# Dividing layer one's first and fifth mixing product into seven, with the shared sums made earlier

## The chip, the cores and the metric

The kernel runs on one core of a Trainium2 chip. The metric is the device time of one execution in microseconds (us); of several runs the median is given. TensorE (PE in the profile) multiplies matrices, VectorE (DVE) and ScalarE (ACT) work elementwise, GpSimd (POOL) does elementwise work and issues some DMAs, and SyncE (SP) issues the other DMAs in one queue.

## The reference

Two layers with the same weights, over a sequence of 2048 tokens with 512 features, all in fp32. Each layer is a linear attention block A and a gated mixer B, both behind a layer norm and with a residual.

```
def A(x):                      # 32 heads of 16
    q, k, v = split(x @ wqkv)
    pq, pk = phi(q), phi(k)    # phi(t) = (t + 1 if t > 0 else exp(t)) + 1e-6
    kv, z = pk^T v, sum_s pk
    return concat_heads((pq @ kv) / (pq @ z + 1e-6)) @ wo

def B(x):                      # 1792 features, halves of 896
    z = gelu(x @ w_in)
    z1, z2 = z[:, :896], layernorm(z[:, 896:])
    g = w_sp @ z2 + b_sp       # w_sp: 2048 x 2048, mixes the tokens
    return (z1 * g) @ w_out

for layer in (1, 2):
    x = x + A(layernorm(x))
    x = x + B(layernorm(x))
```

The term that this study is about is `w_sp @ z2`, called the mixing here.

## The kernel before

Every fp32 operand of a large matmul is split into a high part (ScalarE copies it as fp32r) and a low part (VectorE subtracts); a product is three matmuls, high by high, high by low and low by high (`mm3`, lines 121 to 125, and `acc` in the mixing, lines 1049 to 1053). The order in which each engine gets its instructions is the order of the program, written out by hand. Buffers come from four pools with first-in-first-out lists (class `Slots`): 22 pages of 128 x 512, 6 `quads` of 128 x 2048, 4 `bigs` of 128 x 3584 and 8 banks of PSUM. In the profile these are pg, qd, bg and bank; z tiles hold the normalised z2, 128 tokens each.

A layer has four stages.

- First half (class `P1`), 16 token tiles: layer norm statistics (`stats`: VectorE, then three small operations on GpSimd, lines 190 to 193), normalising on ScalarE (line 199), a store and load through DRAM that, with a blockwise transpose on VectorE (line 251), turns the tile (class `Turn`), and its split (`T_high`, `T_low`). Then the projections K and Q, phi (lines 323 to 327), and the product of x with phi(k) (`Gmm`); step s does K of tile s-1, Q of s-1 and `Gmm` of s-2, 36 matmuls. Before the first tile TensorE is given filler matmuls (`idle` in `start`, line 415).
- `transition`, and the token steps (class `P2`, 18 steps): attention's output (`c`), the next layer norm, the turned x and its split (`d_high`, `d_low`), z2 (`e`, with the Gelu in `e2`, line 667) and z1 (`f`), which is stored to DRAM.
- The mixing (class `P4`): w_sp is a 2 x 2 block matrix, and seven block products (Winograd's form) make up the result. They are called P1 to P7 here and run in the order P2, P1, P6, P7, P4, P5, P3. A product has 8 steps of 24 matmuls (P2, P1, P4, P5) or of 18. Per step `sp` splits the fetched block of w_sp (`wsp`, high on ScalarE in line 885, low on VectorE in line 886) and the z operand (`zsp`), two steps ahead; `fetch` loads four steps ahead. `evac` takes a product's banks out into the big tiles on VectorE. `gate` (line 1089, GpSimd) multiplies a finished unit of g with z1, loaded by `ask`; `tick` issues one gate a step in undivided products.
- The output product with w_out (`o`), to whose steps the next layer's start is joined. P3's steps also load and split w_out (`wpiece`).

`DIVIDED` names the products that are themselves taken as seven products of quarter blocks: 14 steps of 12 matmuls (`mm_div`, `evac_div`), whose z operands are summed and split on VectorE and ScalarE (`zsum`, `zpart`) four steps ahead. Before, this is layer two's P2 and P4.

Sums of blocks of w_sp are needed by both layers (class `Sums`). `tick` makes two of them on GpSimd (`add`, line 805) from loaded blocks and stores them (line 800); the blocks are loaded one call ahead by `fetch`, and if none is loaded `tick` loads them at once. There are 32 such calls, 14 in layer one's token steps and the rest in its mixing. Before, the divided products' sums (`halve`, line 783) are all made in layer one's mixing: 16 copies from DRAM to DRAM on SP, then 16 accumulating DMAs issued by GpSimd (line 795), each behind the newest weight split (`behind` adds such a wait, `self.mark` is that ScalarE instruction).

## Time and profile before

| | |
|---|---|
| time, median of 3 runs | 1388.18 us (1385.9 to 1389.07) |
| the profiled execution | 1386.75 us, span 1384.9 us |
| TensorE busy | 1376.4 us, 6182 matmuls |
| VectorE, ScalarE, GpSimd busy | 893.1, 587.6, 396.7 us |
| DMA | 248.76 MB, mean 180 GB/s |
| layer one's mixing | 351.4 to 624.8 us |
| layer two's mixing | 1041.1 to 1304.6 us |

The profile is one execution. A line of a group gives the source line, the engine and the operation, the tiles written and read, the shape and the count; then busy time, the mean of one in ns, and the idle time just before them with what ended it. A line of the order of time gives the start and the length in us, and in brackets the idle time before the instruction and what released it. A row of stretches gives for each engine the busy time and in brackets the number of instructions.

### The profile page before, as it was taken

Reading aid. Unit: us, or ns where it says so; the run is one execution under the profiler, and the core shown is the slowest. Engines: PE = TensorE matmul, PEld = TensorE weight load, DVE = VectorE, ACT = ScalarE, POOL = GpSimd, SP = SyncE. Lnnn points to the kernel's source line nnn. Section 1 sums busy time; section 2 is a strip of 40 time slices with the busy share of each in tenths; the row PEclk is TensorE's granted clock in tenths of the full one; section 3 lists DMA queues with packets and bytes.
Section 4 is the critical chain, followed back from the end, with each engine's and each line's share of the span. In section 5 each row is a group of like instructions: output and inputs, shape, how many; then the busy total and the mean of one; then the engine's idle time right before and its main releaser. Section 6 shows DMA issues by size and latency. Waiting matters only on the chain.

```text
span 1384.9 us, 17460 instructions
## 1 busy us (share of the span) xinstructions
PE 1376.4 (99%) x6182; PEld 1149.0 (83%) x6182; DVE 893.1 (64%) x1331; ACT 587.6 (42%) x893; POOL 396.7 (29%) x506
## 2 busy tenths in 40 slices
PE   9999999999999999999999999999999999999998
PEld 7888888888888888878888888888888888878887
DVE  6665877752578665674566658775438667886632
ACT  6664534434323333341256646443346333633410
POOL 3333455543466201342012334432100020021300
PEclk9999999999999999999999999999999999999999
DMA  5632267775999877893735322555346445454432
GB/s 159 202 115 62 92 213 258 250 240 193 329 309 317 302 248 190 228 266 114 228 112 185 115 61 95 175 179 168 114 148 202 137 167 155 147 186 149 161 123 91
DMA packets 148344, 248.76 MB, mean 180 GB/s; under 512 B 12448, under 2 KB 51104, under 8 KB 148000
## 3 DMA queue, kind: packets, MB, share of 16 engines
q1 hardware_dynamic: 145952, 239.26, 52.2%
q0 software_dynamic: 2304, 8.39, 3.4%
q8 instruction: 48, 0.79, 0.2%
q14 instruction: 40, 0.33, 0.1%
HBM read 179.70 MB, written 84.67 MB: 191 GB/s over the span
## 4 chain that ended last, share of the span: by engine, by line
PE 91%; DVE 4%; DMA 2%; ACT 2%; issue 1%; POOL 1%; SPq 0%; ACTq 0%; DVEq 0%; POOLq 0%
PE bank L125 18%; PE bank L124 18%; PE bank L123 18%; PE bank L1052 11%; PE bank L1053 11%; PE bank L1051 11%; DMA pg<-in_wout_dram 1%; DVE qd L886 1%; PE bank L515 1%; PE bank L526 0%; ACT qd L885 0%; DVE st L186 0%; PE bank L211 0%; DMA pg<-in_wqkv_dram 0%; DVE pg L112 0%
## 5 line engine op out<-in xcount | busy, mean ns | idle before, releaser
L1052 PE MATMUL bank<-qd,pg 128*128 128x512 f32 x784 | 305.5, 390 | 1.5 <-DVE qd L886 1.5
L1053 PE MATMUL bank<-qd,pg 128*128 128x512 f32 x784 | 305.3, 389 | 0.0
L1051 PE MATMUL bank<-qd,pg 128*128 128x512 f32 x784 | 305.1, 389 | 0.0
L886 DVE TENSOR_TENSOR qd<-qd,qd 128x1024 fp32r<-128x1024 f32 x124 | 166.7, 1345 | 135.3 <-ACT qd L885 135.0
L885 ACT ACTIVATE qd<-qd 128x1024 fp32r<-128x1024 f32 x124 | 131.3, 1059 | 184.4 <-PE bank L1053 158.9
L1052 PEld LDWEIGHTS bank<-qd,pg 128*128 128x128 f32 x784 | 147.1, 188 | 33.9 <-DVE qd L886 3.5
L1053 PEld LDWEIGHTS bank<-qd,pg 128*128 128x128 f32 x784 | 147.2, 188 | 31.1 <-DVE pg L925 0.7
L1051 PEld LDWEIGHTS bank<-qd,pg 128*128 128x128 f32 x784 | 147.1, 188 | 31.0 <-ACT pg L923 0.4
L1089 POOL TENSOR_TENSOR bg<-bg,pg 128x512 f32<-128x512 f32 x56 | 83.8, 1512 | 279.6 <-DVE bg L1099 121.0
L125 PE MATMUL bank<-qd,pg 128*128 128x512 f32 x384 | 149.8, 390 | 0.1
L190 POOL TENSOR_SCALAR rs<-mv 128x1 f32<-128x1 f32 x96 | 27.3, 284 | 343.5 <-DVE mv L188 342.8
L199 ACT ACTIVATE pg<-pg,nb,rs 128x512 f32<-128x512 f32 x63 | 51.2, 812 | 172.1 <-POOL nb L193 172.0
L123 PE MATMUL bank<-qd,pg 128*128 128x512 f32 x288 | 112.4, 390 | 0.1
L124 PE MATMUL bank<-qd,pg 128*128 128x512 f32 x288 | 112.2, 390 | 0.0
L805 POOL TENSOR_TENSOR pg<-pg,pg 128x512 f32<-128x512 f32 x64 | 93.8, 1466 | 55.0 <-DMA pg<-in_wsp_dram 46.0
L123 PE MATMUL bank<-bg,qd 128*128 128x448 f32 x256 | 94.2, 368 | 0.4 <-ACT qd L109 0.4
L125 PE MATMUL bank<-bg,qd 128*128 128x448 f32 x256 | 93.6, 365 | 0.1
L124 PE MATMUL bank<-bg,qd 128*128 128x448 f32 x256 | 93.6, 366 | 0.0
L125 PE MATMUL bank<-qd,bg 128*128 128x512 f32 x224 | 87.5, 391 | 0.0
L124 PE MATMUL bank<-qd,bg 128*128 128x512 f32 x224 | 87.4, 390 | 0.0
L123 PE MATMUL bank<-qd,bg 128*128 128x512 f32 x224 | 87.2, 389 | 0.0
L123 PE MATMUL bank<-wo,qd 128*128 128x512 f32 x224 | 87.1, 389 | 0.0
(137 smaller groups left out, 2557.9 us busy)
## 6 DMA issues: line engine op xcount, KB each, us to landing
qd<-s SPq DMA_DIRECT2D x64, 512.0 KB, 3.8
qd<-in_wsp_dram SPq DMA_DIRECT2D x44, 512.0 KB, 4.2
pg<-in_wsp_dram SPq DMA_DIRECT2D x64, 256.0 KB, 4.8
s<-pg SPq DMA_DIRECT2D x64, 256.0 KB, 4.5
pg<-x SPq DMA_DIRECT2D x64, 256.0 KB, 2.9
z<-pg SPq DMA_DIRECT2D x56, 256.0 KB, 2.8
pg<-z SPq DMA_DIRECT2D x56, 256.0 KB, 4.3
x<-pg SPq DMA_DIRECT2D x48, 256.0 KB, 2.6
```

Of the source, the lines that this page charges most:

```text
L123: nc.tensor.matmul(out, ah, bh, start=start, stop=False)
L124: nc.tensor.matmul(out, ah, bl, start=False, stop=False)
L125: nc.tensor.matmul(out, al, bh, start=False, stop=stop)
L190: nc.gpsimd.tensor_scalar(rs, mv[:, 1:2], LN_EPS, None, op0=OP.add)
L199: nc.scalar.activation(y, x, AF.Identity, bias=nb, scale=rs)
L805: nc.gpsimd.tensor_tensor(t, a, b, op=OP.add)
L885: self.mark = nc.scalar.activation(w[:, 0], r, AF.Copy)
L886: nc.vector.tensor_sub(w[:, 1], r, w[:, 0].bitcast(F32))
L1051: m(out, h[:, o], w[:, 0, j, :], start=start, stop=False, skip_group_check=True)
L1052: m(out, h[:, o], w[:, 1, j, :], start=False, stop=False, skip_group_check=True)
L1053: m(out, l[:, o], w[:, 0, j, :], start=False, stop=stop, skip_group_check=True)
L1089: nc.gpsimd.tensor_tensor(u, u, z1, op=OP.mult)
```

## The change

- Layer one's P2 and P4 are divided too.
- The shared sums start in layer one's first half: eight calls of `tick` in its steps 2 to 9, with two big tiles cut into sheets as their buffers (class `Sheets`), 14 in the token steps as before, none in P2, ten in P1 and P6.
- The divided products' sums are made earlier: the copies for P2 in steps 14 to 17 of the first half, its accumulations in token steps 4 to 11 (behind that step's Gelu), the copies for P4 in token steps 9 to 16, its accumulations in P6 and the start of P7.
- A gate waits for the newest weight split.
- `evac` takes the two delta banks of P1 and P5 out after the others; in layer one P1's banks are taken out ahead of the next split.
- At the end of P7 the weight split of one more step is issued ahead of `evac`. Counters (`made`, `zmade`) keep a split from being made twice.
- `Turn.pre` issues the VectorE transpose of the next tile at the end of a step of the first half.
- The last four filler matmuls are half as wide.

```diff
@@ -50,7 +50,25 @@
             self.free_list.append(n)
 
 
-DIVIDED = ((), ("P2", "P4"))
+DIVIDED = (("P2", "P4"), ("P2", "P4"))
+
+
+class Sheets:
+
+
+    def __init__(self, slots, n):
+        self.slots = slots
+        self.tiles = [slots.get([P, NF, 512]) for _ in range(n)]
+        self.free_list = deque(t[:, f, :] for t in self.tiles for f in range(NF))
+
+    def get(self, shape):
+        return self.free_list.popleft()
+
+    def put(self, *sheets):
+        self.free_list.extend(sheets)
+
+    def close(self):
+        self.slots.put(*self.tiles)
 
 
 @with_exitstack
@@ -217,7 +235,7 @@
 
         def __init__(self, name, by_pe, always=False, inbank=False):
             self.name, self.by_pe, self.always, self.inbank = name, by_pe, always, inbank
-            self.held, self.d, self.raw = {}, {}, {}
+            self.held, self.d, self.raw, self.made = {}, {}, {}, {}
 
         def turned(self, i):
 
@@ -245,12 +263,19 @@
                 if self.always:
                     pages.put(s)
                 return b, banks
+            self.pre(i)
+            return self.made.pop(i)
+
+        def pre(self, i):
+
+            if i in self.made or i not in self.raw:
+                return
             r = self.raw.pop(i)
             home = banks if self.inbank else pages
             y = home.get([P, 4, P])
             nc.vector.transpose(y.rearrange("p c (t m) -> p m c t", m=4), r.rearrange("p (m c j) -> p m c j", m=4, c=4))
             pages.put(r)
-            return y, home
+            self.made[i] = y, home
 
 
     class P1:
@@ -410,9 +435,9 @@
             nc.vector.tensor_copy(m, f)
             b = banks.get(PAGE)
 
-            def idle(n):
+            def idle(n, w=512):
                 for _ in range(n):
-                    nc.tensor.matmul(b, ones, m, start=True, stop=True)
+                    nc.tensor.matmul(b[:, 0:w], ones, m[:, 0:w], start=True, stop=True)
 
             idle(10)
             self.ln_a(0)
@@ -420,7 +445,7 @@
             self.ln_b(0)
             self.wk.piece()
             self.T_high(0)
-            idle(4)
+            idle(4, 256)
             banks.put(b)
             pages.put(m, f)
             self.T_low(0)
@@ -467,10 +492,24 @@
                     self.Gmm(s - 2)
                 if s == NT + 1:
                     self.late_phi()
+                if self.L == 0:
+                    if s == 2:
+                        sums.slots = Sheets(bigs, 2)
+                    if 2 <= s < 10:
+                        sums.tick(s < 9)
+                    if s == 10:
+                        sums.store()
+                        sums.slots.close()
+                        sums.slots = pages
+                    if 14 <= s < 18:
+                        sums.halve(2 * s - 28, None)
+                        sums.halve(2 * s - 27, None)
                 if s == 6:
                     self.wv, self.wo = (quads.get([P, 4, 512]) for _ in range(2))
                     nc.sync.dma_start(self.wv, wqkv[:, 1024:1536].rearrange("(c p) f -> p c f", p=P))
                     nc.sync.dma_start(self.wo, wo_d.rearrange("(c p) f -> p c f", p=P))
+                if s in range(3,NT-1):
+                    self.turn.pre(s + 1)
                 if s > 3 and side:
                     side.popleft().piece()
                 if s > 2 and side:
@@ -664,7 +703,7 @@
         def e2(self, i):
             z = ztag(i, [P, FH], f"z{self.L}")
             for j, b in enumerate(self.eb):
-                nc.scalar.activation(z[:, j * HF:(j + 1) * HF], b, AF.Gelu_apprx_tanh)
+                self.mark = nc.scalar.activation(z[:, j * HF:(j + 1) * HF], b, AF.Gelu_apprx_tanh)
                 banks.put(b)
 
         def e3(self, i):
@@ -747,8 +786,13 @@
                 self.fnext = []
                 w1.piece(True)
                 w1.fetch()
-                if self.L == 0 and s > 4:
-                    sums.tick()
+                if self.L == 0:
+                    if s > 4:
+                        sums.tick(s < NT + 2)
+                    if 4 <= s < 12:
+                        sums.halve(12 + s, self.mark)
+                    if 9 <= s < 17:
+                        sums.halve(s - 1, None)
                 if s >= NT + 1:
                     self.p4.fetch(s - NT - 1)
             self.e4(NT - 1)
@@ -847,6 +891,7 @@
                 else:
                     self.steps += [(p, k) for k in range(HT)]
             self.tmp, self.bank = {}, {}
+            self.made = 0
             self.beta = self.delta = None
             self.wout = {}
             self.asked, self.gq = deque(self.gates()), deque()
@@ -873,9 +918,11 @@
             self.raw[g] = t
 
         def sp(self, g):
-            self.wsp(g)
-            if g < len(self.steps) and self.steps[g][0] not in self.div:
-                self.zsp(g)
+            while self.made < min(g + 1, len(self.steps)):
+                self.wsp(self.made)
+                if self.steps[self.made][0] not in self.div:
+                    self.zsp(self.made)
+                self.made += 1
 
         def wsp(self, g):
             if g >= len(self.steps):
@@ -1086,20 +1133,13 @@
         def gate(self, n, f):
             z1 = self.z1.pop((n, f))
             u = self.unit(n, f)
-            nc.gpsimd.tensor_tensor(u, u, z1, op=OP.mult)
+            behind(nc.gpsimd.tensor_tensor(u, u, z1, op=OP.mult), self.mark)
             pages.put(z1)
 
         def evac(self, p):
 
             V, bs = nc.vector, self.bs
             gates = []
-            if p in ("P1", "P5"):
-                for j in range(2):
-                    n = 2 + j if p == "P1" else j
-                    V.tensor_add(self.unit(n, 3), self.unit(n, 3) if self.joins(p) else bs[n],
-                                 self.delta[j])
-                    gates.append((n, 3))
-                banks.put(*self.delta)
             for j in range(2):
                 a, b = 2 + j, j
                 for f in range(3):
@@ -1126,6 +1166,13 @@
                         gates.append((a, 4 + f))
                     if p in ("P2", "P4", "P3") or (p == "P7" and "P4" in self.div):
                         banks.put(q)
+            if p in ("P1", "P5"):
+                for j in range(2):
+                    n = 2 + j if p == "P1" else j
+                    V.tensor_add(self.unit(n, 3), self.unit(n, 3) if self.joins(p) else bs[n],
+                                 self.delta[j])
+                    gates.append((n, 3))
+                banks.put(*self.delta)
             self.gq.extend(gates)
 
         def wpiece(self, f):
@@ -1163,27 +1210,25 @@
             if i % 4 == 3:
                 bigs.put(self.gb[i // 4])
 
+        def zahead(self, g):
+
+            while self.zmade <= g:
+                self.zsum(self.zmade + 1)
+                self.zpart(self.zmade)
+                self.zmade += 1
+
         def run(self, nxt):
             p2 = self.p2
             self.fetch(2)
             self.sp(0)
             if self.div:
                 self.loadb()
-            ahead = deque()
+            self.zmade = 0
             if self.div:
-                self.zpart(0)
-                self.zpart(1)
-                ahead.extend([2, 3, 4, 5, 6, 7][:4 - 2])
-                self.zsum(2)
+                self.zahead(1)
             while p2.f():
-                if ahead:
-                    g = ahead.popleft()
-                    self.zsum(g + 1)
-                    self.zpart(g)
-            while ahead:
-                g = ahead.popleft()
-                self.zsum(g + 1)
-                self.zpart(g)
+                self.zahead(min(self.zmade, 3))
+            self.zahead(3)
             p2.win1.free()
             self.sp(1)
             self.fetch(3)
@@ -1192,20 +1237,25 @@
             for g in range(n):
                 p, k = self.steps[g]
                 self.fetch(g + 4)
-                evac_first = p == "P6" and k == HT - 1
+                evac_first = (p == "P6" or p == "P1" and nxt is not None) and k == HT - 1
                 div_first = p in self.div and k == 13 and p == "P4"
                 if not evac_first and not div_first:
                     self.sp(g + 2)
-                    self.zsum(g + 4 + 1)
-                    self.zpart(g + 4)
+                    self.zahead(g + 4 if p in ("P2", "P1") else g + 4)
                 self.mm(g)
                 if evac_first:
+                    if p == "P1":
+                        self.ask(3)
                     self.evac(p)
                     self.sp(g + 2)
-                if g < 19:
+                if p != "P2" or not self.div:
                     self.sums.tick()
-                if nxt is not None:
-                    self.sums.halve(g - 19, self.mark)
+                elif nxt is not None and k == 1:
+                    self.sums.store()
+                elif nxt is not None and k == 13:
+                    self.sums.fetch()
+                if nxt is not None and g >= 24:
+                    self.sums.halve(g, self.mark)
                 if g == 3 and not self.div:
                     self.loadb()
                 if p in self.div:
@@ -1227,6 +1277,8 @@
                         self.loadx(1)
                     if k == 7:
                         self.zsplit(0)
+                if p == "P7" and k == HT - 1 and self.div:
+                    self.sp(g + 3)
                 if k == HT - 1 and not evac_first:
                     self.evac(p)
             pages.put(*self.bs)
```

## The prediction

> **What bounds the kernel now.** I read the page first (busy shares, the chain that ended last, the costly groups), then busy time by stretches of the span, then the waits and the order of time around each stall. The page:
>
> ```profile
> span 1384.9 us, 17460 instructions
> PE 1376.4 (99%) x6182; PEld 1149.0 (83%) x6182; DVE 893.1 (64%) x1331; ACT 587.6 (42%) x893; POOL 396.7 (29%) x506
> PE 91%; DVE 4%; DMA 2%; ACT 2%; issue 1%; POOL 1%; SPq 0%; ACTq 0%; DVEq 0%; POOLq 0%
> L1052 PE MATMUL bank<-qd,pg 128*128 128x512 f32 x784 | 305.5, 390 | 1.5 <-DVE qd L886 1.5
> L805 POOL TENSOR_TENSOR pg<-pg,pg 128x512 f32<-128x512 f32 x64 | 93.8, 1466 | 55.0 <-DMA pg<-in_wsp_dram 46.0
> ```
>
> TensorE is busy for 99% of the span and makes 91% of the chain. The L1052 row is one of the mixing's three matmul lines (L1051 to L1053); it waited 1.5 us in all over both layers. L805 are the shared sums' adds on GpSimd, 1.47 us each, which waited 46 us for their blocks. So a matmul taken away is worth its pace, unless something else becomes late.
>
> The two layers run the same mixing, but layer two takes P2 and P4 (the first and fifth block product, in the order P2, P1, P6, P7, P4, P5, P3) as seven half-size products already. The trace of before therefore shows the changed stage once. First the matmuls of line L1051 in the mixing of layer one and of layer two, then all engines in single products. The columns after the stretch are its length, the busy time of each engine with its instruction count, TensorE's granted clock, the DMA share and GB/s.
>
> ```profile
> 351.40:624.80 273.40, 155.61 (x400) 74.92 (x400) 1.00 0.86 271
> 1041.10:1304.60 263.50, 149.52 (x384) 71.91 (x384) 1.00 0.51 167
> ```
> ```profile
> 351.40:395.10 43.70, 43.70 (x195) 36.18 (x194) 28.98 (x29) 14.75 (x19) 21.43 (x14) 1.00 0.96 333
> 395.10:438.70 43.60, 43.60 (x194) 36.12 (x193) 32.53 (x32) 12.47 (x16) 24.63 (x16) 1.00 0.93 310
> 1041.10:1079.30 38.20, 38.20 (x169) 31.33 (x169) 34.58 (x53) 24.06 (x34) 0.00 (x0) 1.00 0.67 209
> 1079.30:1122.90 43.60, 43.60 (x194) 36.12 (x193) 25.67 (x39) 12.46 (x16) 1.67 (x2) 1.00 0.39 131
> 1122.90:1155.70 32.80, 32.80 (x147) 27.15 (x146) 20.96 (x27) 11.51 (x15) 8.80 (x7) 1.00 0.51 176
> 1188.40:1228.40 40.00, 39.25 (x171) 31.30 (x169) 37.34 (x56) 24.93 (x37) 4.83 (x3) 1.00 0.54 171
> ```
>
> The first two of the second block are P2 and P1 of layer one, the other four P2, P1, P6 and P4 of layer two. Undivided P2 takes 43.7 us, divided 38.2; divided P4 40.0, because it has stalls. The reader should see what the division costs beside TensorE: VectorE works 34.6 of 38.2 us and 37.3 of 40.0, against 29.0 of 43.7 undivided. That is narrow, and it holds only while GpSimd does next to nothing (0.0 and 4.8 us there, 21 to 25 us in layer one's first two products).
>
> **The matmuls removed.** An undivided P2 or P4 has 8 steps of 24 matmuls, 192; divided it has 14 steps of 12, 168. Two products save 48, as the rows say: 400 less 384 is 16 on each of three lines. The pace is 43.7 us / 192 = 0.2276 us in the undivided product and 38.2 / 168 = 0.2274 in the divided one. 48 x 0.2274 = **-10.9 us**, all on the path.
>
> **Stalls that the change may take away.** The first blocks are TensorE's own order of time at late matmuls, then ScalarE's, GpSimd's and VectorE's beside them.
>
> ```profile
> 615.31 0.39 PE L1051 MATMUL bank<-qd,pg 128*128 128x512 f32 x1
> 616.49 0.50 PE L1052 MATMUL bank<-qd,pg 128*128 128x512 f32 x1 [0.79 <-DVE qd L886]
> ```
> ```profile
> 1194.56 0.50 PE L1052 MATMUL bank<-qd,pg 128*128 128x512 f32 x1 [0.45 <-DVE qd L886]
> ...
> 1219.64 0.50 PE L1052 MATMUL bank<-qd,pg 128*128 128x512 f32 x1 [0.30 <-DVE qd L886]
> ```
> ```profile
> 1188.68 3.62 ACT L1117 ACTIVATE bg<-bg 128x512 f32<-128x512 f32 x6 [2.64 <-DVE bg L1115]
> ```
> ```profile
> 1213.70 3.53 POOL L1089 TENSOR_TENSOR bg<-bg,pg 128x512 f32<-128x512 f32 x2 [70.24 <-DVE bg L1017]
> ```
> ```profile
> 1210.46 1.22 DVE L886 TENSOR_TENSOR qd<-qd,qd 128x1024 fp32r<-128x1024 f32 x1
> ...
> 1214.14 1.95 DVE L886 TENSOR_TENSOR qd<-qd,qd 128x1024 fp32r<-128x1024 f32 x1
> ```
>
> In layer two's P4 the stall at 1194 follows six ScalarE copies (L1117, the end of P7) that stand ahead of the next weight split; the change puts that split ahead of them. The one at 1219 follows two gates (L1089) that GpSimd began inside P4: beside them the split's low half took 1.95 us and not 1.22. The change makes a gate wait for the ScalarE half of the newest split, which holds it back until P5. Both stalls have an answer, so of the 40.0 - 38.2 = 1.8 us that P4 loses I take 1.5 back (bounds 0 and 1.8): **-1.5 us**. Queued behind a gate that waits are only GpSimd's later gates, and on SP the load into the page that it frees. The late matmul at 615, in layer one's P3, is (616.49 - 615.31) - 0.23 = 0.95 us late; it came while accumulating DMAs and P3's loads of w_out shared the DMA engines. The accumulating DMAs move ahead to P6 and P7, but P3's gates now wait for splits; I take 0.8 back (bounds +1 and -0.95): **-0.8 us**.
>
> **The sums' cold starts.** A tick that finds no loaded blocks holds GpSimd until they land. Before, this happens once, in the token steps; the rows are GpSimd, ScalarE and TensorE there.
>
> ```profile
> 191.61 2.66 POOL L805 TENSOR_TENSOR pg<-pg,pg 128x512 f32<-128x512 f32 x2 [3.07 <-DMA pg<-in_wsp_dram]
> ```
> ```profile
> 195.64 0.82 ACT L199 ACTIVATE pg<-pg,nb,rs 128x512 f32<-128x512 f32 x1 [8.07 <-POOL nb L193]
> ```
> ```profile
> 196.28 0.39 PE L125 MATMUL bank<-qd,pg 128*128 128x512 f32 x1
> 197.03 0.47 PE L123 MATMUL bank<-bg,qd 128*128 128x448 f32 x1 [0.36 <-ACT qd L109]
> ```
> ```profile
> L795 POOL DMA_DIRECT2D hP<-in_wsp_dram x8 | 6.8, 853 | 84.9 <-ACT qd L885 84.9
> ```
>
> GpSimd waits 3.07 us for the blocks, the layer norm's statistics stand behind the adds, ScalarE's normalising behind them, and a matmul is 0.52 us late. The change keeps this cold tick and puts an accumulating DMA behind its adds (0.85 us of GpSimd, L795) ahead of the same statistics. Its wait for the step's Gelu costs nothing: on GpSimd it stands behind the statistics of that Gelu's output. **+0.8 us** (bounds 0 and 3; the upper end if the blocks land later beside the accumulation).
>
> The second cold tick is new, in layer one's first half at its second step.
>
> ```profile
> 29.04 0.22 POOL L190 TENSOR_SCALAR rs<-mv 128x1 f32<-128x1 f32 x1 [2.12 <-DVE mv L188]
> ```
> ```profile
> 25.69 0.38 SPq L235 DMA_DIRECT2D xt<-pg  x1
> ```
> ```profile
> pg<-in_wsp_dram SPq DMA_DIRECT2D x64, 256.0 KB, 4.8
> ```
> ```profile
> 35.37 0.69 DVE L112 TENSOR_TENSOR pg<-bank,pg 128x512 fp32r<-128x512 f32 x1
> ```
> ```profile
> 40.14 0.39 PE L123 MATMUL bank<-qd,pg 128*128 128x512 f32 x1
> ```
>
> The loads go out behind the store at 25.69, the third about 27; landing takes 4.8 us, so both adds (2.66) are done near 34.4, and the statistics that ran at 29.04 start 5.4 us late. From them a serial chain (normalise, phi, turn, split) ends in the L112 of 35.37, done at 36.06, which the matmul at 40.14 needs: 4.1 us of slack. 5.4 - 4.1 = 1.3; I take **+1.0 us** (bounds 0 and 3). The later ticks load one step ahead (36 matmuls, 8.2 us, against 4.8) and are hidden. A tick's store waits on SP for the adds; behind it stand the next x load and turned load, needed a step later.
>
> **The traffic that moves.**
>
> ```profile
> 18.20:82.00 63.80, 63.80 (x284) 52.79 (x283) 43.44 (x74) 44.33 (x75) 19.35 (x32) 1.00 0.52 163
> 115.00:148.00 33.00, 33.00 (x160) 26.58 (x159) 19.83 (x39) 15.50 (x28) 8.89 (x8) 1.00 0.13 43
> 194.00:352.00 158.00, 157.57 (x723) 135.28 (x722) 93.00 (x141) 64.19 (x104) 77.59 (x111) 1.00 0.72 237
> ```
> ```profile
> q0 software_dynamic: 2304, 8.39, 3.4%
> ```
>
> Eight ticks with 8.4 MB of loads and stores go to the stretch from 18 to 82 us. At 333 GB/s for a share of 0.96 they are 24 us of DMA, 3 a tick and 0.38 of the stretch: 0.52 becomes 0.90. Eight copies of 0.5 MB go to the end of the first half (share 0.13), eight to the token steps, with eight accumulations (3.4% of 1384.9 us / 16 = 2.9 us each; a token step's 60 matmuls are some 13): 0.72 becomes about 0.94, more for three steps where both fall. No matmul waited at 0.96 in layer one's P2, so I cost this at nothing. If the cover is gone, the token steps' turned loads come late. VectorE has room for the adds: 43.4 of 63.8 us, plus 16 times the 0.73 us by which a busy GpSimd lengthened a split, is 55.
>
> The Trainium skill, "SBUF — State Buffer", section "Who interferes with whom", says that a VectorE instruction with two SBUF inputs and a GpSimd one that reads SBUF exclude each other for the whole instruction. The rows agree that they hurt each other, by 0.73 us and not by the whole of a gate. Its outcome is a rival below.
>
> In layer one's mixing the accumulations for P4 fall in P6 and early P7, ten ticks in P1 and P6, and P1's results are now taken out, by eight VectorE operations, ahead of the next split. For all that together: **+0.8 us** (bounds 0 and 4). The turn issued at the end of the step before, the two delta banks taken out last in P1 and P5, and the counters for splits and parts change an order only where today no matmul waits, and the next step's 18 to 36 matmuls cover them: 0.
>
> **The warm-up.**
>
> ```profile
> 7.22 1.16 PE L415 MATMUL bank<-pg,ones 128*128 128x512 f32 x4
> 8.53 0.51 PE L123 MATMUL bank<-qd,pg 128*128 128x512 f32 x1
> ```
>
> Four half-width filler matmuls save some 0.45 us, but the first real matmul already starts after their end, waiting for its split: 0 (bounds -0.4 and +0.5).
>
> **Sum:** -10.9 - 1.5 - 0.8 + 0.8 + 1.0 + 0.8 = -10.6 us. The profiled execution took 1386.75 us (span 1384.9 and 1.85 around it), so 1376.15; the median of the runs, 1388.18, lies 1.43 above it: **1377.6 us**.
>
> **Rivals.**
> *P6 becomes bound by DMA* (15%). Layer two's P6 has a share of 0.51, 16.7 us of 32.8. Six accumulations add 17.6 and two ticks about 6: 40 us, 7.5 too many. Fetched blocks have two steps (36 matmuls, 8.2 us) less some 4.8 of landing, 3.4 us, so 4.1 us would be lost: 1381.7. For it: the sum of shares. Against: P1 of layer one ran at 0.93 without a wait, and the accumulations may be what waits.
> *Slower: the ticks starve the layer norm in the first half* (9%). If the adds' blocks land later than 8.2 + 4.1 = 12.3 us, every tick delays the statistics, and GpSimd, ScalarE and TensorE in turn. Slower than before by 0.2% needs 13.4 us of new loss, 1.7 us in each of eight steps, a landing of 14.0. At three times today's 4.8 (14.4) it would be 2.1 x 8 = 17 us: 1394. For it: a share near 0.90 on average, with 2 MB of weights in the middle. Against: the 64 loads of the 4.8 us ran in stretches with shares of 0.72 to 0.96.
> *VectorE is shut out for the whole of each add* (6%), the rule named above. 16 adds in P1 of layer one at 1.47 us are 23.5 us on top of layer two's P1, 25.7 of 43.6, 5.6 over; in the first half 43.4 + 23.5 is 3.1 over 63.8; 8.7 lost: 1386.3, no change. Against: layer one's P1 today, VectorE 32.5 and GpSimd 24.6 of 43.6, with no wait.
> That the matmuls are not saved is excluded by the count.
>
> **How the numbers follow.** The forecast's case has 70%. About 0.2%, 2.8 us, is what a measurement of this kernel tells from no change. The forecast and the first rival are faster (0.85), the third the same (0.06), the second slower (0.09). Low end: all stalls gone, nothing new, -10.9 - 1.8 - 0.95 - 0.4 = -14.1, 1374.1, less 1.6 for the runs' spread. High end: the first rival, 1381.7, with the two cold ticks some 1.2 us dearer each, 1384.
>
> **What would show it.** Right: 384 matmuls on each mixing line in layer one and a mixing of 262 to 264 us there; layer two's P4 near 38.2; waits of 0.5 to 2 us near 40 and 197. Wrong: TensorE waiting in every step from 24 to 82 us, in P6, or VectorE over 38 us in layer one's divided products.

## The result and the profile after

The changed kernel takes 1402.32 us in the median of four runs (1400.12 to 1403.28), the kernel before 1387.10 in four. The ratio is 1.0106, with a 95% interval from 1.0088 to 1.0125: 15 us slower, where 10.6 us faster was forecast. The profiled execution took 1400.12 us.

The page of the changed kernel: its span, the busy shares, TensorE's granted clock in 40 slices, and the chain that ended last, by engine and by line.

```profile
span 1398.3 us, 17506 instructions
PE 1373.8 (98%) x6134; PEld 1142.9 (82%) x6134; DVE 937.7 (67%) x1411; ACT 611.4 (44%) x939; POOL 420.1 (30%) x506
PEclk9999999899999999999999999999999999999999
PE 82%; DMA 7%; DVE 5%; ACT 2%; POOL 1%; issue 1%; SPq 1%; DVEq 0%; ACTq 0%; POOLq 0%
PE bank L141 15%; PE bank L143 15%; PE bank L142 15%; PE bank L1099 12%; PE bank L1098 12%; PE bank L1100 12%; DMA yt<-pg 2%; DMA s<-pg 2%; DMA pg<-xt 1%; DVE st L204 1%; DMA qd<-s 1%; DVE pg L130 1%; ACT pg L217 1%; PE bank L554 1%; DMA z<-pg 0%
```

The 48 matmuls are gone (6134, before 6182), TensorE is busy 2.6 us less, and yet the span is 13.4 us longer. DMA had 2% of the chain and has 7%, and the chain names the transfers: the store of the turned tile in the token steps (yt), the store of a finished sum (s). One slice of the clock row, the eighth (245 to 280 us), is not a 9.

The stretches tell where. First the kernel before, then the changed one, each with the first half and transition, layer one's token steps, layer one's mixing and layer two's mixing. The columns are the length, busy time and count of PE, PEld, DVE, ACT and POOL, the granted clock, the DMA share and GB/s.

```profile
2.30:159.10 156.80, 156.53 (x704) 127.98 (x705) 104.89 (x184) 94.69 (x160) 50.63 (x77) 1.00 0.41 128
159.10:351.50 192.40, 191.97 (x892) 165.68 (x891) 120.90 (x189) 79.49 (x129) 95.45 (x137) 1.00 0.69 224
351.50:624.80 273.30, 272.51 (x1202) 225.09 (x1201) 190.02 (x218) 94.82 (x123) 101.19 (x73) 1.00 0.86 271
1041.20:1304.60 263.40, 262.65 (x1154) 215.72 (x1153) 198.34 (x288) 117.67 (x164) 33.76 (x24) 1.00 0.51 167
```
```profile
2.30:160.90 158.60, 156.35 (x705) 127.12 (x705) 106.90 (x184) 95.05 (x161) 75.27 (x93) 1.00 0.64 206
160.90:375.10 214.20, 199.95 (x890) 169.54 (x889) 117.69 (x199) 80.71 (x134) 97.30 (x142) 0.96 0.80 242
375.10:640.50 265.40, 263.42 (x1154) 215.65 (x1154) 224.36 (x287) 116.97 (x164) 81.75 (x52) 1.00 0.70 223
1056.80:1318.20 261.40, 261.40 (x1153) 216.21 (x1152) 209.04 (x288) 117.91 (x164) 49.07 (x24) 1.00 0.51 168
```

Layer one's mixing is 7.9 us shorter and layer two's 2.0, the first half is 1.8 longer, and the token steps are **21.8 us longer**; the remaining stretches are unchanged. In the token steps TensorE stands still for 14.3 us (before 0.4), and nearly the same number of matmuls takes 8.0 us longer. Only there is the granted clock below 1.00.

The largest group of TensorE's waits in the whole span (total, times, longest), and the order of time around the longest: TensorE, then VectorE, ScalarE, and the issues of SP and GpSimd. The last fence is the same store and load in the kernel before.

```profile
PE bank L141 <- ACT qd L127: 13.9, 5, 6.7
```
```profile
238.25 0.40 PE L143 MATMUL bank<-qd,pg 128*128 128x512 f32 x1
245.40 0.74 PE L141 MATMUL bank<-bg,qd 128*128 128x448 f32 x1 [6.74 <-ACT qd L127]
...
233.25 1.10 DVE L276 STREAM_TRANSPOSE pg<-pg 128x512 f32<-128x512 f32 x1 [3.15 <-DMA yt<-pg]
243.60 1.08 DVE L276 STREAM_TRANSPOSE pg<-pg 128x512 f32<-128x512 f32 x1 [5.49 <-DMA s<-pg]
...
244.71 0.63 ACT L127 ACTIVATE qd<-pg 128x512 fp32r<-128x512 f32 x1 [4.65 <-DVE pg L276]
...
226.73 0.37 SPq L253 DMA_DIRECT2D yt<-pg  x1
233.22 0.32 SPq L118 DMA_DIRECT2D pg<-yt  x1
...
234.01 0.93 POOL L839 DMA_DIRECT2D hP<-hP  x1
```
```profile
220.21 0.37 SPq L235 DMA_DIRECT2D yt<-pg  x1
222.69 0.32 SPq L100 DMA_DIRECT2D pg<-yt  x1
```

All of the 13.9 us end with the split of the turned tile (L127), the operand of z2's matmuls (L141). Read the longest wait backwards: the split waits for the transpose at 243.60, the transpose for a DMA, and before that the load could not go out until the store had landed, 6.5 us after it was issued; before it was 2.5. The transpose at 243.60 is put down to the store of a sum (s): the load it reads had landed at 236.0, 2.8 us after its issue, but the page it writes to came free only when that store was done, 8 to 9 us after its issue at 234.6, beside the accumulating DMA (hP<-hP) issued at 234.01. The transpose at 233.25 turns another tile (attention's) and is put down to yt's store in the same way.

The second longest wait (3.29 us, at 277.75) ends with a sum's store too. In the other three (1.23 us at 199.62, 0.81 at 227.28, 1.85 at 305.19) the split stands on ScalarE right behind a normalising that waited for GpSimd's statistics, in the last two of them because VectorE was late behind such pages. The lines give what VectorE's transposes waited for (total, times, longest), first in the kernel before (180 to 300 us), then in the changed one (190 to 320 us).

```profile
DVE pg L251 <- DMA yt<-pg: 0.7, 2, 0.5
```
```profile
DVE pg L276 <- DMA yt<-pg: 14.0, 4, 4.9
DVE pg L276 <- DMA s<-pg: 11.7, 2, 6.2
DVE pg L276 <- DMA pg<-yt: 0.3, 1, 0.3
```

It is the stores that VectorE waits for there, for the pages under them, and hardly the load. So a token step is a loop in which one store, one load and the return of pages to the pool follow each other, and its matmuls wait for the end of it.

The DMA view of 195 to 352 us gives the count, the size and the median time from issue to landing. The first line is the kernel before, the others the changed one.

```profile
yt<-pg SPq DMA_DIRECT2D x11, 256.0 KB, 2.8
```
```profile
hP<-in_wsp_dram SPq DMA_DIRECT2D x8, 512.0 KB, 6.2
yt<-pg SPq DMA_DIRECT2D x11, 256.0 KB, 5.9
pg<-yt SPq DMA_DIRECT2D x11, 256.0 KB, 2.9
hP<-hP POOLq DMA_DIRECT2D x4, 512.0 KB, 9.2
hP<-in_wsp_dram POOLq DMA_DIRECT2D x3, 512.0 KB, 8.0
```

The store lands in twice the time; the load behind it does not. A mean share of 0.80 hides how the transfers lie within a step. Stretches of 2 us, in the changed kernel:

```profile
222.00:224.00 2.00, 2.00 (x10) 1.68 (x9) 1.93 (x4) 0.00 (x0) 0.00 (x0) 1.00 1.22 254
226.00:228.00 2.00, 1.15 (x5) 0.34 (x3) 0.69 (x1) 2.00 (x3) 1.09 (x1) 1.00 1.00 238
232.00:234.00 2.00, 2.00 (x11) 1.69 (x10) 0.75 (x1) 0.00 (x0) 1.92 (x2) 1.00 0.07 22
```

A step sends its transfers off together; the engines are then full (a share at or over 1.00) and afterwards nearly idle (0.07). The store goes out while they are full, at 226.73. Full stretches as such are not new: before, the shares from 224 to 232 us were 0.95, 1.03, 1.00 and 1.06, but the store of 220.21 went out ahead of them, in a stretch at 0.85. These rows show that store and full engines now coincide, not yet that the one delays the other.

### The profile page after: what moved, and what is told of

Same layout as the page of the kernel before. It is cut to its first block, busy times and chain, and to the rows that moved or that the text cites. A ratio compares the mean times of both kernels' runs of the same rounds, so it can differ in the third digit from the quotient of the medians.

```text
span 1398.3 us, 17506 instructions
## 1 busy us (share of the span) xinstructions
PE 1373.8 (98%) x6134; PEld 1142.9 (82%) x6134; DVE 937.7 (67%) x1411; ACT 611.4 (44%) x939; POOL 420.1 (30%) x506
## 4 chain that ended last, share of the span: by engine, by line
PE 82%; DMA 7%; DVE 5%; ACT 2%; POOL 1%; issue 1%; SPq 1%; DVEq 0%; ACTq 0%; POOLq 0%
PE bank L141 15%; PE bank L143 15%; PE bank L142 15%; PE bank L1099 12%; PE bank L1098 12%; PE bank L1100 12%; DMA yt<-pg 2%; DMA s<-pg 2%; DMA pg<-xt 1%; DVE st L204 1%; DMA qd<-s 1%; DVE pg L130 1%; ACT pg L217 1%; PE bank L554 1%; DMA z<-pg 0%
## 5 line engine op out<-in xcount | busy, mean ns | idle before, releaser
L1098 PE MATMUL bank<-qd,pg 128*128 128x512 f32 x768 | 299.1, 389 | 1.9 <-DVE bg L1153 1.2
L1099 PE MATMUL bank<-qd,pg 128*128 128x512 f32 x768 | 299.3, 390 | 0.0
L1100 PE MATMUL bank<-qd,pg 128*128 128x512 f32 x768 | 299.2, 390 | 0.1
L933 DVE TENSOR_TENSOR qd<-qd,qd 128x1024 fp32r<-128x1024 f32 x136 | 175.3, 1291 | 92.7 <-ACT qd L932 92.4
L932 ACT ACTIVATE qd<-qd 128x1024 fp32r<-128x1024 f32 x136 | 143.7, 1057 | 165.7 <-PE bank L1100 93.3
L1136 POOL TENSOR_TENSOR bg<-bg,pg 128x512 f32<-128x512 f32 x56 | 106.1, 1903 | 363.4 <-ACT qd L932 327.7
L1098 PEld LDWEIGHTS bank<-qd,pg 128*128 128x128 f32 x768 | 144.2, 188 | 32.7 <-ACT qd L932 1.6
L1099 PEld LDWEIGHTS bank<-qd,pg 128*128 128x128 f32 x768 | 144.2, 188 | 31.2 <-DVE qd L933 1.6
L1100 PEld LDWEIGHTS bank<-qd,pg 128*128 128x128 f32 x768 | 144.2, 188 | 31.0 <-DVE pg L974 0.8
L143 PE MATMUL bank<-qd,pg 128*128 128x512 f32 x384 | 149.9, 390 | 0.1
L141 PE MATMUL bank<-qd,pg 128*128 128x512 f32 x288 | 112.8, 392 | 2.2 <-DVE pg L130 2.0
L142 PE MATMUL bank<-qd,pg 128*128 128x512 f32 x288 | 112.3, 390 | 0.0
L141 PE MATMUL bank<-bg,qd 128*128 128x448 f32 x256 | 97.0, 379 | 13.9 <-ACT qd L127 13.9
L143 PE MATMUL bank<-bg,qd 128*128 128x448 f32 x256 | 96.4, 377 | 0.2
L142 PE MATMUL bank<-bg,qd 128*128 128x448 f32 x256 | 95.8, 374 | 0.0
L849 POOL TENSOR_TENSOR pg<-pg,pg 128x512 f32<-128x512 f32 x48 | 68.4, 1424 | 72.5 <-DVE pg L972 55.2
L141 PE MATMUL bank<-qd,bg 128*128 128x512 f32 x224 | 87.2, 389 | 0.0
L141 PE MATMUL bank<-wo,qd 128*128 128x512 f32 x224 | 87.1, 389 | 0.0
```

Source lines behind the costliest of these rows:

```text
L141: nc.tensor.matmul(out, ah, bh, start=start, stop=False)
L142: nc.tensor.matmul(out, ah, bl, start=False, stop=False)
L143: nc.tensor.matmul(out, al, bh, start=False, stop=stop)
L849: nc.gpsimd.tensor_tensor(t, a, b, op=OP.add)
L932: self.mark = nc.scalar.activation(w[:, 0], r, AF.Copy)
L933: nc.vector.tensor_sub(w[:, 1], r, w[:, 0].bitcast(F32))
```

## The experiments

What had to be told apart: whether the transfers that moved into the token steps cost the time (by their bytes, their place in SP's queue, or GpSimd's part in them), or something else in the change; and how much the late operand itself costs, against the slower clock behind it. The stretches are those of one profiled execution of each kernel, which need not lie at the median: the changed kernel's is 2.2 us below its own, that of the copies moved 4.0 and that of the copies on another queue 4.3 (1394.49 against 1398.75). Gains read from such stretches are uncertain by about 2 us.

**Thin accumulations.** The token steps' accumulating DMAs move 16 of 128 partitions, so the sums for layer one's P2 are incomplete.

```diff
-sums.halve(12 + s, self.mark)
+sums.halve(12 + s, self.mark, True)
...
+if thin:
+    dst, src = dst[:, 0:16], src[:, 0:16]
```

> The changed kernel, but the eight accumulating DMAs of the token steps move 16 of 128 partitions, an eighth of their bytes; GpSimd issues as many, at the same places (layer one's P2 sums are then incomplete). Theory T, the bytes of these DMAs keep the turned x's store from landing: layer one's token steps, 214 us in the changed kernel, fall to 196 to 202, the time to 1384 to 1390. Theory U, GpSimd's own 0.9 us for issuing each of them ahead of the layer norm's statistics: token steps stay over 210, the time near 1402. Theory C, the copies alone stretch the stores: token steps 206 to 212.

Measured: 1395.98 us, 1.0074 of before [1.0049, 1.0099]; token steps 207.0 us. The token steps lie between theories T and U, in the range given for theory C, the copies alone (206 to 212). But an eighth of the bytes brings back 7 of the 21.8 us, so the accumulations' bytes are part of it too, and GpSimd's issues, which all stayed, can't be the whole. Most of the loss remains, and the store still landed in 5.8 us.

**Copies moved to the mixing.** The copies for P4 leave the token steps for the first eight steps of layer one's P2.

```diff
-if 9 <= s < 17:
-    sums.halve(s - 1, None)
...
+if nxt is not None and g < 8:
+    self.sums.halve(8 + g, None)
```

> The changed kernel with the eight copies for P4 moved out of the token steps into the first eight steps of layer one's P2; the accumulations stay. Theory T: the stalls near 198, 226 and 238 us stay, those near 274 and 303 shrink; token steps 203 to 209 us, time 1391 to 1397. Theory C (the copies are the cause): token steps 193 to 197, time 1381 to 1385. Theory U: token steps over 210.

Measured: 1399.12 us, 1.0089 [1.0068, 1.0109]; token steps 206.6 us, the mixing 2.5 longer than in the changed kernel. The token steps fell as theory T had it (203 to 209); the time came out above its range (1391 to 1397). The copies have about the same part as the accumulations' bytes, and neither alone is the cause.

**Both moved.** In addition the copies for P2 go out in steps 10 to 12 of the first half and its accumulations in steps 13 to 16, so that, with the copies for P4 moved as above, none of this traffic is left in the token steps.

```diff
-if 14 <= s < 18:
-    sums.halve(2 * s - 28, None)
-    sums.halve(2 * s - 27, None)
+if 10 <= s < 13:
+    for n in range(3 * s - 30, min(3 * s - 27, 8)):
+        sums.halve(n, None)
+if 13 <= s < 17:
+    sums.halve(2 * s - 10, self.last)
+    sums.halve(2 * s - 9, self.last)
...
-if 4 <= s < 12:
-    sums.halve(12 + s, self.mark)
```

> The changed kernel with the copies for P4 in layer one's P2 and the accumulations for P2 in steps 13 to 16 of the first half (their copies in steps 10 to 12). All theories that blame something in the token steps: these fall to 193 to 196 us. T: the first half bears the traffic, because its turned load has a step more of room: at most 2 us more there, time 1380 to 1384. U: the first half loses what the token steps gain, since GpSimd's statistics stand behind the issues there too: time over 1390.

Measured: 1389.2 us, 1.0012 [0.9998, 1.0027]. First half, token steps, mixing:

```profile
2.30:168.10 165.80, 160.20 (x704) 128.30 (x705) 106.97 (x184) 94.44 (x160) 82.04 (x101) 0.99 0.72 222
168.10:360.60 192.50, 191.81 (x891) 165.66 (x890) 124.95 (x199) 81.25 (x134) 91.57 (x134) 1.00 0.69 225
360.60:629.70 269.10, 264.83 (x1153) 216.81 (x1152) 227.60 (x288) 117.41 (x164) 84.47 (x52) 0.99 0.72 236
```

The token steps are back at 192.5 us (before 192.4): the whole loss there belongs to this traffic. But it takes its price along. The first half, which has the same loop through DRAM (xt), loses 7.2 us against the changed kernel at a mean share of 0.72, not the 2 that theory T allowed; VectorE's turn waited up to 4.8 us for a load of xt there. The mixing is 3.7 us longer than in the changed kernel.

**Before, with the traffic alone.** The kernel before with only these transfers put where the change puts them: copies and accumulations for P2, copies for P4; the products stay undivided.

```diff
+if self.L == 0 and 14 <= s < 18:
+    sums.halve(2 * s - 28, None)
+    sums.halve(2 * s - 27, None)
...
+if self.L == 0 and 4 <= s < 12:
+    sums.halve(12 + s, self.mark)
+if self.L == 0 and 9 <= s < 17:
+    sums.halve(s - 1, None)
```

> The kernel before, undivided in layer one, with only the token-step traffic of the change: copies for P2 at the end of the first half, its accumulations and the copies for P4 in the token steps. T: the token steps grow from 192 to 207 to 216 us and the time from 1387 to 1402 to 1411. Theory V, the loss comes from another part of the change (the sums started in the first half, the order of splits, the earlier turn): time 1385 to 1390.

Measured: 1409.5 us, 1.0166 [1.0149, 1.0183]; token steps 211.1 us against 192.4, with the store landing in 6.0 us. The traffic alone makes 18.7 of the 21.8 us, without divided products, sheets or tied gates. The mixing of this kernel takes 277.3 us, 4.0 more than before, for which no run gives the reason.

**Copies on another queue.** In the changed kernel ScalarE issues all 16 copies, so that none stands ahead of the store in SP's queue.

```diff
-nc.sync.dma_start(self.halves[p, m, q], src)
+nc.scalar.dma_start(self.halves[p, m, q], src)
```

> The changed kernel with its sixteen copies issued from ScalarE's queue instead of SP's; places, sizes and accumulations are the same. Theory T1, what is queued on SP behind a copy waits for the whole copy: the turned x's stores of the late token steps land in 2.5 to 4 us again and not in 5.5 to 8.5, layer one's token steps fall from 214 to 205 to 208 us, the time to 1392 to 1396. Theory T2, the copies hurt by their bytes, whatever queue they are on: stores still over 5 us, token steps 211 to 216, time 1399 to 1405.

Measured: 1398.75 us, 1.0081 [1.0059, 1.0104]; token steps 207.9 us, the store landing in 5.0 us (changed kernel 5.9, before 2.8). The copies' place in SP's queue is worth some 6 of the 21.8 us by the stretches, 3.6 by the medians; the token steps came out as theory T1 had it, the store's landing and the time did not. The store is also late when none of them stands ahead of it on its own queue; what remains isn't that order.

**No round trip.** In the changed kernel TensorE turns the first twelve tiles of the token steps itself, not four; all the traffic stays.

```diff
-Turn(f"yt{L}", range(4))
+Turn(f"yt{L}", range(12) if L == 0 else range(4))
```

> The changed kernel, but in layer one's token steps tiles 4 to 11 of the new x are turned by TensorE, as tiles 0 to 3 are, and not through DRAM; all its traffic stays. If the loss runs through the turned x's store and load, token steps fall from 214 to 196 to 201 us (192.3 before, and 8 times four small matmuls of 0.11 us), time 1384 to 1389. If the late transfers act elsewhere too (attention's turned tiles, the x loads, the sums' loads), token steps stay over 205.

Measured: 1382.31 us, 0.9967 [0.9956, 0.9978]. Token steps and mixing:

```profile
161.10:355.80 194.70, 194.70 (x922) 168.95 (x921) 110.82 (x191) 82.07 (x134) 97.97 (x142) 1.00 0.80 244
355.80:625.20 269.40, 264.40 (x1154) 217.80 (x1153) 224.97 (x288) 117.63 (x164) 83.98 (x52) 0.99 0.68 220
```

At the same share of 0.80 TensorE no longer waits at all in the token steps; with 32 small transposes more the stage is 2.3 us longer than before the change. That is shorter than expected. So a high DMA share alone did not slow the stage: the tile's way through DRAM has to be there too. But the one line takes away more than the store and the load. Their 4 MB are gone from the stage, the two pages that the load and the transpose took stay in the pool, and the kernel issues the split of a tile that TensorE turns ahead of the step's normalising and not behind it (`late` in the class `P2`): ScalarE's split no longer stands behind GpSimd's statistics, as it did in three of the five waits. Which of these did how much was not separated; more pages, or a page of its own for the transposed tile, would be the next experiment. The mixing is 4 us longer than in the changed kernel, above all by one wait of 4.8 us for VectorE between P6 and P7, where the accumulations for P4 run.

**Fillers in the waits.** 24, 14 and 8 matmuls of 448 columns, whose result nobody reads, stand ahead of z2's matmuls in the three steps with the longest waits.

```diff
+if self.L == 0 and s in (10, 12, 14):
+    fb, fw = banks.get([P, HF]), self.win2.h
+    for _ in range({10: 24, 12: 14, 14: 8}[s]):
+        nc.tensor.matmul(fb, fw[:, 0, 0:P], fw[:, 0, 0:HF], start=True, stop=True)
+    banks.put(fb)
```

> The changed kernel with filler matmuls ahead of z2's matmuls in the three token steps with the longest waits (24, 14 and 8 of 448 columns, some 4.8, 2.8 and 1.6 us, in waits of 6.9, 3.5 and 2.0 us). Theory H, a wait of 2 us and more lets TensorE's clock fall to half, and the matmuls after it run at half pace: the matmuls 0.17 us late each vanish behind the second and third wait at least, the waits themselves stay, time 1.5 to 5 us below the changed kernel's 1402. Otherwise the pace behind the waits stays, time 1402 to 1406.

Measured: 1397.79 us, 1.0084 [1.0064, 1.0104]; token steps 209.5 us. The changed kernel's stretch after its longest wait, then the order of time with fillers:

```profile
245.40:252.00 6.60, 6.60 (x19) 5.76 (x20) 5.74 (x9) 2.95 (x5) 3.42 (x5) 0.55 0.65 214
```
```profile
237.84 5.03 PE L782 MATMUL bank<-bg 128*128 128x448 f32 x24
244.01 0.47 PE L141 MATMUL bank<-bg,qd 128*128 128x448 f32 x1 [1.14 <-ACT qd L127]
244.31 0.37 PE L142 MATMUL bank<-bg,qd 128*128 128x448 f32 x1
```

Without fillers the clock is 0.55 for 6.6 us after the wait, and 19 matmuls begin in that time; with them the first two matmuls after the wait take 0.47 and 0.37 us, not 0.74 and 0.57, and the clock of the run is 1.000. The stage is 4.7 us shorter than the changed kernel's with as many late operands: some 5 of the 21.8 us are the half clock behind a wait, and the other 17 or so the late operands themselves. (The matmuls took 8.0 us longer in the changed kernel; a part of that would have been waiting anyway.) The Trainium skill, "TensorE: Matmul & The Clock Gate", Part 1, section "What's actually happening", gives half rate after an idle window of about 3.4 us, with a window that runs on freely. The longest wait agrees; behind one of 1.85 us, below that figure, the clock was at half too, as the changed kernel's order of time and the stretch from that matmul on show:

```profile
305.19 0.47 PE L141 MATMUL bank<-bg,qd 128*128 128x448 f32 x1 [1.85 <-ACT qd L127]
```
```profile
305.19:309.20 4.01, 3.95 (x11) 3.23 (x12) 2.04 (x4) 2.32 (x4) 0.83 (x3) 0.59 1.02 370
```

The length of the wait does not decide alone at this size. In the 3 to 4 us behind waits of 1.49 us (thin accumulations), 1.51 (copies on another queue), 1.68 and 1.80 (copies moved) the granted clock was 0.56 to 0.72; behind 1.68 (transfers placed anew), 1.70 and 2.02 (before, with the traffic alone) and 1.90 (copies on another queue) it was 1.00.

**Untied gates.** The changed kernel without the gate's wait for the newest split.

```diff
-behind(nc.gpsimd.tensor_tensor(u, u, z1, op=OP.mult), self.mark)
+nc.gpsimd.tensor_tensor(u, u, z1, op=OP.mult)
```

> The changed kernel with its gates no longer tied to the splits. If the gates inside layer two's P4 made the wait near 1219 us: layer two's mixing, 261.4 us in the changed kernel and 263.4 before, comes back by 0.5 to 1.0 us, with VectorE's weight splits of 1.9 us beside the gates again. If only the split moved ahead of P7's results counted: 261.4 as before. Too small for the time to tell.

Measured: 1402.74 us, 1.0110 [1.0093, 1.0128], no different as a whole. Layer two's mixing and one of its splits:

```profile
1059.00:1322.10 263.10, 262.65 (x1154) 215.84 (x1153) 199.10 (x288) 117.97 (x164) 34.92 (x24) 1.00 0.51 167
```
```profile
1231.60 1.95 DVE L933 TENSOR_TENSOR qd<-qd,qd 128x1024 fp32r<-128x1024 f32 x1
```

The mixing takes 263.1 us, against 261.4 with the tie and 263.4 before, and the split beside the gates again takes 1.95 us. The tie is worth 1.7 of the 2.0 us that layer two gained, in one execution of each; 0.5 to 1.0 was expected.

**Transfers placed anew.** The changed kernel with its accumulations for P2 in the first half's last steps and the token steps 1, 2 and 4, at whose start TensorE turns the tiles; the copies for P4 in the token steps 13 to 16; its accumulations four steps later, in P7; blocks loaded ahead of the first tick of each stage; the 2 MB of weights at step 12 of the first half, not 6.

```diff
-if 2 <= s < 10:
+    sums.fetch()
+if 3 <= s < 11:
...
-if 4 <= s < 12:
-    sums.halve(12 + s, self.mark)
-if 9 <= s < 17:
-    sums.halve(s - 1, None)
+if s in (1, 2, 4):
+    for n in {1: (18, 19), 2: (20, 21), 4: (22, 23)}[s]:
+        sums.halve(n, None)
+if 13 <= s < 17:
+    sums.halve(2 * s - 18, None)
+    sums.halve(2 * s - 17, None)
...
-if nxt is not None and g >= 24:
-    self.sums.halve(g, self.mark)
+if nxt is not None and g >= 28:
+    self.sums.halve(g - 4, self.mark)
```

> The changed kernel with its transfers placed where no turned tile is in flight or where there is room: P2's accumulations at the end of the first half and in token steps 1, 2 and 4 (tiles turned by TensorE), P4's copies in token steps 13 to 16, P4's accumulations four steps later (mostly P7), the sums' first blocks loaded ahead of the first tick in both places, and 2 MB of weights after the first half's ticks. T: token steps 192 to 195 us, first half 157 to 159, mixing 262 to 265, time 1372 to 1378, under both kernels. If the division itself costs TensorE's waits in layer one's mixing: mixing over 267, time over 1380.

Measured: 1381.94 us, 0.9965 [0.9955, 0.9976]; token steps 196.1 us, mixing 264.1, first half 159.3. Token steps, first half and time missed what was expected, by 1, 0.3 and 4 us; the mixing met it. Of the token steps' loss 18 us come back, with all eight copies and six of the eight accumulations still in the stage, the tiles turned as in the changed kernel and the order of the splits unchanged. So where the transfers lie makes most of the loss.

**Two edits.** No round trip, and the accumulations for P4 four steps later; nothing else of the above.

```diff
-Turn(f"yt{L}", range(4))
+Turn(f"yt{L}", range(12) if L == 0 else range(4))
...
-if nxt is not None and g >= 24:
-    self.sums.halve(g, self.mark)
+if nxt is not None and g >= 28:
+    self.sums.halve(g - 4, self.mark)
```

> The changed kernel with two edits: tiles 4 to 11 of the token steps turned by TensorE, and P4's accumulations issued four steps later, so that six of the eight lie in P7. If P6's late fetches come from the accumulations beside them: layer one's mixing falls from 269.4 us (with the first edit alone) to 263 to 265, the time from 1382.3 to 1375 to 1378. If its stall is VectorE's or belongs to the division itself: mixing over 267, time 1380 to 1384.

Measured: 1379.22 us, 0.9940 [0.9928, 0.9952]; token steps 194.7, mixing 265.6. The wait at P6's end is gone, so the accumulations made it; two matmuls came late early in P4 (0.9 and 1.0 us), so the mixing missed its expectation a little.

**The version that beats both.** The transfers placed anew, eight tiles turned by TensorE, and the 2 MB of weights in eight parts.

```diff
-Turn(f"yt{L}", range(4))
+Turn(f"yt{L}", range(8) if L == 0 else range(4))
...
+if self.L == 0 and 6 <= s < 14:
+    c = (s - 6) % 4
+    r = slice(c * P, (c + 1) * P)
+    if s < 10:
+        nc.sync.dma_start(self.wv[:, c], wqkv[r, 1024:1536])
+    else:
+        nc.sync.dma_start(self.wo[:, c], wo_d[r, :])
```

> The kernel with its transfers placed anew, with tiles 4 to 7 of the token steps turned by TensorE too and the 2 MB of attention's weights loaded in eight parts, one a step from 6 to 13. Token steps 193 to 195 us, first half 157.0 to 158.5, mixing 262 to 264.5, time 1374 to 1379. If the stalls near 199 and 214 us in the token steps came from GpSimd and not from the turned tiles: token steps over 197.

Measured: **1378.40 us, 0.9936 [0.9924, 0.9947]**. First half, token steps, mixing:

```profile
2.30:159.90 157.60, 156.62 (x703) 128.15 (x704) 107.42 (x186) 94.82 (x161) 77.47 (x97) 1.00 0.69 218
159.90:354.90 195.00, 193.49 (x908) 167.26 (x906) 118.69 (x193) 81.81 (x134) 95.35 (x138) 1.00 0.78 246
354.90:617.00 262.10, 261.76 (x1154) 216.10 (x1153) 225.68 (x288) 117.51 (x164) 85.32 (x52) 1.00 0.71 226
```

All four met their expectation. The share in the token steps is 0.78, against 0.80 in the changed kernel; the stage is 19 us shorter. The store there lands in 3.5 us.

## Why the prediction was wrong, step by step

**The step that failed is "The traffic that moves".** It took the token steps' share to about 0.94, compared it with 0.96 in layer one's P2, where no matmul waited, and cost it at nothing. The share came out at 0.80 of the longer stage (the same transfers would be 0.89 of the 192.4 us before), and the stage lost 21.8 us. The comparison was of two unlike things. The mixing loads its blocks four steps ahead, so that a transfer may take several times its usual time unseen; a token step sends a tile to DRAM and back for its own next matmuls and works in pages that come free only when stores have landed. There yt's store took 5.9 us in place of 2.8, a sum's store 8 to 9 in the longest wait, and TensorE stood still for 14.3 us in place of 0.4. The sentence on the lost cover came close to what then happened ("the token steps' turned loads come late"; it was the stores, the load itself took 2.9 us as before) and gave it neither a price nor a chance; the range ended 18 us below the result. What ought to have been read was the 2.5 us from yt's store to its load, which pages wait for a store, how much longer either might take before z2's matmuls wait, and the share by bursts of a few us. The slower rival was of this kind, transfers that starve a serial chain, but it stood in the first half and went through GpSimd, and its end, 1394, was lower too.

**The matmuls removed** were right: 768 on each mixing line over both layers, so 384 in layer one, as foreseen.

```profile
L1098 PE MATMUL bank<-qd,pg 128*128 128x512 f32 x768 | 299.1, 389 | 1.9 <-DVE bg L1153 1.2
```

**Layer two's P4**: 1.5 us forecast; the mixing gained 2.0, and it has no stall left (261.40 us busy of 261.40). The untied run bears out the gates' part of the mechanism (1.7). The stall at 615 in layer one's P3, 0.8 forecast, is gone too.

**The cold starts.** In the token steps 0.8 was forecast; the matmul at 199.62 waited 1.23 us, by the way foreseen (blocks, adds, statistics, normalising), and the step lost about 0.9 more than before. In the first half 1.0 was forecast, and no matmul waited near 40 us: the statistics behind the cold adds began at 33.03 us and not at 34.4, 4.0 us later than before, within the 4.1 of slack. But another matmul came late where nothing was foreseen, and the stage lost 1.8:

```profile
199.62 0.47 PE L141 MATMUL bank<-bg,qd 128*128 128x448 f32 x1 [1.23 <-ACT qd L127]
...
74.34 0.50 PE L141 MATMUL bank<-qd,pg 128*128 128x512 f32 x1 [1.59 <-DVE pg L130]
...
71.53 0.73 DVE L276 STREAM_TRANSPOSE bank<-pg 128x512 f32<-128x512 f32 x1 [4.94 <-DMA pg<-xt]
```

That is again a turned load, behind the 2 MB of weights and a tick's blocks: the same mechanism, small. With the weights in parts, and the ticks' blocks loaded a step ahead, the stage takes 157.6 us.

**Layer one's mixing**, +0.8 forecast within bounds of 0 and 4: it lost about 3.0 more than that, 3.8 us in all (265.4 us against 273.3 - 10.9 - 0.8). Most of it is at P6, the place of the first rival, in a fetched block (a sum, s) that lands late, as that rival had it, and in P6's results being taken out late behind the splits.

```profile
492.34 0.47 PE L1098 MATMUL bank<-qd,pg 128*128 128x512 f32 x1 [1.21 <-DVE bg L1153]
482.19 1.06 ACT L932 ACTIVATE qd<-qd 128x1024 fp32r<-128x1024 f32 x1 [6.22 <-DMA qd<-s]
```

Its sum gave 4.1 us for P6; two matmuls, at 492 and 497 us, came 2.2 us late together. In the experiment with two edits the wait at this place, 4.8 us in the kernel without the round trip, went away when the accumulations for P4 were moved; that they made it here too is likely, not shown.

**VectorE shut out during each add** did not happen: in layer one's P1, with eight ticks (16 adds), TensorE had no wait of its own.

```profile
413.30:457.20 43.90, 43.90 (x195) 36.22 (x194) 38.21 (x38) 13.85 (x18) 27.19 (x17) 1.00 0.95 322
```

VectorE is busy 38.2 us there, 12.5 more than in layer two's P1 (25.7, in the kernel before), and the rival had added 23.5; TensorE runs without a gap, at a share of 0.95. So the rival's sum, every add to its full length, was too high. The rule that it followed (the Trainium skill, "SBUF — State Buffer", "Who interferes with whom") is about single instructions that overlap, and a row over a whole product neither bears it out nor refutes it.

All in all: 13.4 us longer in the span, against 10.6 shorter: 24 us apart. About 21 of them are the token steps, 3 layer one's mixing and 0.8 the first half, less 0.5 that layer two gave more.

**What stays open.** Why the 256 KB store lands so late is known only in part. Queue order is a share of it, and an eighth of the accumulated bytes left its median at 5.8 us though the stage got 7 us shorter. Whether the engines share by transfer, by packet or by the order of writes to DRAM was not separated. That the moved traffic makes the token steps' loss is shown; by which way is in part argued. The trace puts the two longest waits, 10.0 of the 13.9 us, to pages under a sum's store, but no run had more pages, another order of them, or the split in its new place with the tile still going through DRAM.

## What to carry to other kernels

A mean DMA share says nothing about a stage in which a store and the load of the same data lie between two steps' work: read there the time from the store's issue to the load's, its slack, the buffers that come free only when a store has landed, and the share in bursts. Extra transfers belong where operands are fetched steps ahead (0.95 was harmless in P1, though P6 lost some 2 us at 0.92; 0.80 cost 21 us here), or the round trip has to go. A wait of some microseconds on TensorE can be paid again in a half clock behind it: some 5 of the 21.8 us here.

## What was not expected of the hardware

- An accumulating DMA from DRAM to DRAM of 512 KB took 8.0 to 9.2 us to land beside this traffic, and one of 64 KB on 16 partitions still 6.2 to 7.6.
- A copy of 512 KB on ScalarE's queue still left the stores on SP's at 5.0 us, where they take 2.8 without it and the accumulations.
- After a wait of 1.85 us TensorE's next matmuls ran at half pace already, after one of 2.02 us in another run they did not; the granted clock after the longest wait was 0.55 over 6.6 us.
- TensorE's transposes of eight more tiles (32 small matmuls) cost 2.3 us of the stage, less than one of the longer waits for the way through DRAM.
